# Splitting the last 2048 columns of one weight load into rows of 96, 20 and 12 partitions, and issuing four small loads ahead of the opening barrier

## Chip, cores, metric

One core of a Trainium2 chip. The metric is the device time of one execution in microseconds (us). Intervals are 95% intervals.

## The reference, cut

One decode step of a gated mix: attention of 32 query heads over 4 key/value heads with 65,536 cached positions, and a small gMLP mixer.

```python
q = (x @ wq)...; scores = einsum(q, k) * Dh ** (-0.5); p = softmax(scores)
a = einsum(p, v) @ wo                      # k_cache, v_cache: 4 x 65536 x 128 bf16 each
z = gelu(x @ w_in); z1, z2 = z[:Fh], layernorm(z[Fh:])
b = (z1 * (w_sp @ z2 + b_sp)) @ w_out      # w_out: 1792 x 1024
out = g * a + (1 - g) * b                  # g = sigmoid((x * gate_w).sum())
```

Some 162 MB have to be read for a result of 1,024 numbers.

Of the kernel before, what the change touches and what calls it, by code (L numbers as in the profile page):

```python
# [18 lines left out]
def handle_set(handle):  # L19
    return OrderedEngineSet([handle.engine])  # L20


class Recorder:
# [4 lines left out]
    def __init__(self):  # L28
        self.ops = []
        self.writer = {}  # L30
        self.readers = {}
        self.dma_count = {}
        self.ahead = 0
        self.at = None

    def op(self, eng, fn, r=(), w=(), dma=None, chan=None, take=()):
        o = Op()
        o.eng, o.fn, o.inc, o.count = eng, fn, False, 0
        o.dma, o.chan, o.take = None, chan, take
        o.at = self.at if eng == "PE" else None  # L40
        deps = {}
        for k in r:
            if k in self.writer:
                deps[id(self.writer[k])] = (self.writer[k], True)
        for k in w:
            if k in self.writer:
                deps.setdefault(id(self.writer[k]), (self.writer[k], False))
            for x in self.readers.get(k, ()):
                deps.setdefault(id(x), (x, False))
        o.deps = list(deps.values())  # L50
        for k in r:
            self.readers.setdefault(k, []).append(o)
        for k in w:
            self.writer[k] = o
            self.readers[k] = []
        if dma is not None:
            self.dma_count[dma] = self.dma_count.get(dma, 0) + 16
            o.dma = (dma, self.dma_count[dma])
        o.idx = len(self.ops)
        self.ops.append(o)  # L60
        return o
# [56 lines left out]
    def emit(self, nc):  # L118
        waits = self.plan()
        sems = {e: nc.alloc_semaphore("eng_" + e) for e in self.ENGINES}  # L120
        dsem = {k: nc.alloc_semaphore("dma_%s" % k) for k in self.dma_count}
        final = {k: v for k, v in self.dma_count.items()}

        csem = {c: nc.alloc_semaphore("chan_" + c) for c in {o.chan for o in self.ops if o.chan and o.dma is None}}
        csem.update({o.chan: dsem[o.dma[0]] for o in self.ops if o.chan and o.dma})
        step = {o.chan: 16 if o.dma else 1 for o in self.ops if o.chan}

        def one(o, ws, handle):
            for d in ws:
                if d.dma:  # L130
                    handle.wait_ge(dsem[d.dma[0]], d.dma[1])
                else:
                    handle.wait_ge(sems[d.eng], d.count)  # L133
            for c in o.take:
                handle.wait_ge(csem[c], step[c]).then_inc(csem[c], -step[c])  # L135
            last = o.fn(handle)
            if o.dma:
                last.then_inc(dsem[o.dma[0]], 16)
            elif o.chan:
                last.then_inc(csem[o.chan], 1)  # L140
            elif o.inc:
                last.then_inc(sems[o.eng], 1)

        def run(eng, handle):
            todo = [(o, ws) for o, ws in zip(self.ops, waits) if o.eng == eng]
            looped = [x for x in todo if x[0].at]
            n0 = todo.index(looped[0]) if looped else len(todo)
            assert all(x[0].at for x in todo[n0:n0 + len(looped)])
            for x in todo[:n0]:
                one(*x, handle)  # L150
            if looped:
                parts = {}
                for x in looped:
                    parts.setdefault(x[0].at, []).append(x)
                outer = 1 + max(k[0] for k in parts)
                inner = 1 + max(k[1] for k in parts if k[1] != "end")
                for o in range(outer):
                    for i in [-1] + list(range(inner)) + ["end"]:
                        p, q = parts[(o, i)], parts[(0, min(i, 0) if i != "end" else i)]
                        assert [x[0].take for x in p] == [x[0].take for x in q]  # L160
                with handle.bass.Fori(0, outer, engines=handle_set(handle), head_slot={handle.engine: 0}):
                    for x in parts[(0, -1)]:
                        one(*x, handle)
                    with handle.Fori(0, inner):
                        for x in parts[(0, 0)]:
                            one(*x, handle)
                    for x in parts[(0, "end")]:
                        one(*x, handle)
            for x in todo[n0 + len(looped):]:
                one(*x, handle)  # L170

        body = nc.cur_bb.bb
        gate = next(i for i, x in enumerate(body.instructions)
                    if isinstance(x, mybir.InstDrain) and x.engine == mybir.EngineType.SP)
        first = len(body.instructions)
        run("SP", nc.sync)
        nc.sync.wait_ge(dsem["out"], final["out"])
        made = list(body.instructions)
        moved = made[first:first + self.ahead]
        assert all(isinstance(x, mybir.InstDMACopy) for x in moved)  # L180
        body.instructions = made[:gate] + moved + made[gate:first] + made[first + self.ahead:]
        run("POOL", nc.gpsimd)
        run("ACT", nc.scalar)
        run("DVE", nc.vector)
        run("PE", nc.tensor)


def bass_gated_mix__gqa_block_cached__mixer_gmlp__decode_kernel(
# [45 lines left out]
    OFF = {}  # L234
# [16 lines left out]
    arena = nc.alloc_sbuf_tensor("arena", [128, NA], BF16)  # L251
# [51 lines left out]
    R = Recorder()  # L303
    P = R.op
# [48 lines left out]
    stream = []  # L353
# [1 line left out]

    GRAN = 1024

    def load(keys, src, off, chan=None):

        n = len(stream)  # L360
        w = src.shape[1]
        for i, key in enumerate(keys):
            place[key] = (n, off + i * (w // len(keys)), w // len(keys))
        stream.append((keys, off, src, chan))

    def rows(w, i, c):

        return w[128 * c * i:128 * c * (i + 1), :].rearrange("(p c) n -> p (c n)", c=c)
# [10 lines left out]
    VB = KR * SUB  # L379

    def load_k(n, slot):
        load([("k", n)], kv(A_k_cache, n), slot * SUB)

    def load_k2(n, slot):
        load([("k", n), ("k", n + 1)], kv(A_k_cache, n, True), slot * SUB)

    def load_v2(n, off, chan=None):
        load([("v", n), ("v", n + 1)], kv(A_v_cache, n, True), off, chan)
# [3 lines left out]
    load([("win", 0)], rows(B_w_in, 0, 8), VB)  # L392
    load_k(2, 2)
    load_k(3, 0)
    load([("wout", 0)], rows(B_w_out, 0, 14), VB)
    for i in range(6):
        a = 2 * i + 4
        if i % 3 == 2:
# [17 lines left out]
    def store():  # L416
        P("SP", lambda e: e.dma_start(out[0, 0].rearrange("(q n) -> q n", n=QW), osrc), r=["orow"],
          w=["out"], dma="out")
# [5 lines left out]
    def grains(off, w):  # L424
        return list(range(off // GRAN, (off + w + GRAN - 1) // GRAN))

    def issue():

        while issued[0] < len(stream):
            n = issued[0]  # L430
            keys, off, src, chan = stream[n]
            w = src.shape[1]
            gr = grains(off, w)
            if any(k not in used for x in gr if x in owner for k in owner[x]):
                return
            for j, x in enumerate(gr):
                owner[x] = (keys[j * len(keys) // len(gr)],)
            if n == len(stream) - 1:
                store()
            P("SP", lambda e, o=OFF["RING"] + off, w=w, src=src: e.dma_start(arena[:, o:o + w], src),  # L440
              w=[("slot", x) for x in gr], dma=chan or "s%d" % gr[0], chan=chan)
            issued[0] += 1

    def use(key):
        n, off, w = place[key]
        assert n < issued[0], key
        return arena[:, OFF["RING"] + off:OFF["RING"] + off + w], [("slot", x) for x in grains(off, w)]

    def done(key):
        used.add(key)  # L450
        issue()

    issue()


# [8 lines left out]
      r=["m32"], w=["sel"])  # L464
    P("DVE", lambda e: e.tensor_reduce(mq, vw(idf, 0, [[1, 16], [16, 8]]), AXX, ALU.add), r=["idf"], w=["mq"])
    P("DVE", lambda e: e.tensor_reduce(mhalf, vw(idf, 0, [[32, 2], [64, 2], [1, 32]]), mybir.AxisListType.XY, ALU.add),
      r=["idf"], w=["mhalf"])
# [4 lines left out]
    for fe in range(4):  # L472
        P("POOL", lambda e, fe=fe: e.tensor_copy(vw(sele, 128 * fe, [[32, 4], [1, 32]]),
                                                vw(idb, 64 * (fe // 2) + fe % 2, [[0, 4], [2, 32]])),
          r=["idb"], w=[KSE])
# [5 lines left out]
    def f(e):  # L481
# [7 lines left out]
      r=["oneb", "wsp", "bsp"], w=["mb"])  # L489
# [6 lines left out]
      r=["ones", "gs"], w=[KTB])  # L496
# [4 lines left out]
      r=["g"], w=["omg"])  # L501
# [3 lines left out]
    wqs, keys = use(("wq", 0))  # L505
# [354 lines left out]
    store()  # L860

    R.ahead = 2
    R.emit(nc)


# [26 lines left out]
```

## The kernel before, where the change touches it

All big loads stand in one list, `stream`. SP issues them in that order, each as one copy to all 128 partitions, as soon as the buffer is free. Each instruction is recorded with what it reads and writes; waits follow from that.

```python
def load(keys, src, off, chan=None):
    n = len(stream)
    w = src.shape[1]
    for i, key in enumerate(keys):
        place[key] = (n, off + i * (w // len(keys)), w // len(keys))
    stream.append((keys, off, src, chan))

def rows(w, i, c):                 # c rows of the weight side by side in a partition
    return w[128 * c * i:128 * c * (i + 1), :].rearrange("(p c) n -> p (c n)", c=c)
# ... cut ...
load([("wout", 0)], rows(B_w_out, 0, 14), VB)          # 128 rows of 28,672 bytes
# ... cut ...
P("SP", lambda e, o=OFF["RING"] + off, w=w, src=src: e.dma_start(arena[:, o:o + w], src),
  w=[("slot", x) for x in gr], dma=chan or "s%d" % gr[0], chan=chan)
```

SP's first two loads are moved ahead of the opening barrier already (`R.ahead = 2`). ACT issues four small loads (two of 8 rows of 256 bytes, two scalars of 2 bytes) after it.

## Time and profile before

| | before |
|---|---|
| median of the first 3 runs | 381.98 us (381.87 to 382.19) |
| span of the profiled run | 380.3 us |
| bytes read | 162.01 MB |
| DMA share, 96 to 375 us | 1.00 |
| first part of the last output-weight block lands | 376.48 us |

The profile page has one row per engine in 40 slices, then the DMA queues with packets, megabytes and their share of 16 engines' time. The chain of waits goes back from the last instruction. A table of time windows (the prediction calls them stretches) gives busy times of each engine, then granted clock, DMA share and GB/s. It counts a packet where it starts, so short windows can show a share over 1. Engines go by short names: SP (SyncE, which issues the big loads), ACT (ScalarE), PE (TensorE), DVE (VectorE), POOL (GpSimd).

Where this text speaks of packet records, they are the trace's list of DMA packets: start, duration, size. I speak of the *stretch* of a run: the sum, over the big loads' packets that start between 84 and 90 us, of duration minus the usual duration of that size (2,420 ns for 65,536 bytes, 1,062 for 28,672, 912 for 24,576, 159 for 4,096, 84 for 2,048, 9 for a completion packet of 4). It sums over the sixteen engines, so 16 engine-microseconds are 1 us for each. The kernel before has 0.7 engine-microseconds of it. The records don't name the engine of a packet; where a packet is put down to an engine, it was found by following ends to starts.

### The profile page before, as it was taken

The page shows a single profiled execution, that of the slowest core. Times are in us where ns is not written, and L with a number is a line of the kernel's source. Part 1 is how long each engine was busy: PE and PEld are TensorE (multiplying, and loading weights), DVE is VectorE, ACT ScalarE, POOL GpSimd, SP SyncE. Part 2 cuts the span into 40 slices and gives each one's busy share as a digit, 9 for nine tenths or more (in the row PEclk, how much of TensorE's full clock was granted, in tenths as well). Part 3 has the DMA queues.
Part 4 walks back from the last instruction along what each step waited for, and adds up shares of the span by engine and source line. Part 5 has one row for each costly group of instructions (what it writes and reads, how often), then busy time and mean ns, then how long its engine had stood idle before and what let it go on. Part 6 is the DMA issues. An engine that isn't in the chain of part 4 may idle for free. (4 is left out here: it accounts for less than half of the span.)

```text
span 380.3 us, 2726 instructions
## 1 busy us (share of the span) xinstructions
PE 236.0 (62%) x1477; PEld 60.7 (16%) x861; DVE 205.7 (54%) x166; ACT 23.2 (6%) x24; POOL 8.5 (2%) x39
## 2 busy tenths in 40 slices
PE   0050488466648934895787238953995784649386
PEld 0010011011201210121112001111111111212024
DVE  3111597778379625965892248745874882312020
ACT  1000000010400020002001100020002000220010
POOL 5000000000000000000000000000000000000000
PEclk9997599798959995999699758985899898959789
DMA  9998999999999999999999999999999999999995
GB/s 441 441 420 379 469 388 438 441 490 411 402 415 441 441 441 434 441 396 427 479 441 441 441 414 414 414 441 441 441 424 420 458 441 434 441 400 433 400 433 242
DMA packets 4251, 162.11 MB, mean 426 GB/s; under 512 B 533, under 2 KB 533, under 8 KB 789
## 3 DMA queue, kind: packets, MB, share of 16 engines
q1 hardware_dynamic: 4208, 162.01, 98.9%
q8 instruction: 5, 0.08, 0.1%
q10 hardware_dynamic: 36, 0.00, 0.0%
q14 instruction: 2, 0.01, 0.0%
HBM read 162.01 MB, written 0.00 MB: 426 GB/s over the span
## 5 line engine op out<-in xcount | busy, mean ns | idle before, releaser
L552 DVE STREAM_TRANSPOSE arena<-arena 128x2048 f32<-128x2048 f32 x64 | 143.1, 2285 | 43.9 <-DMA arena<-in_A_k_cache_dram 29.1
L309 PE MATMUL scp<-arena 128*128 128x512 bf16 (+1 forms) x275 | 111.2, 421 | 81.9 <-PEq L135 55.1
L311 PE MATMUL scp<-arena 128*128 128x512 bf16 (+1 forms) x279 | 111.1, 417 | 0.0
L309 PE MATMUL obt<-arena 128*64 128x512 bf16 (+3 forms) x337 | 64.2, 412 | 18.4 <-DMA arena<-in_A_v_cache_dram 11.2
L311 PE MATMUL obt<-arena 128*64 128x512 bf16 (+3 forms) x337 | 63.7, 409 | 0.0
L309 PEld LDWEIGHTS scp<-arena 128*128 128x128 bf16 (+1 forms) x275 | 27.5, 103 | 194.1 <-issue 170.5
L604 DVE STREAM_TRANSPOSE arena<-arena 128x2048 bf16<-128x2048 bf16 x7 | 16.2, 2311 | 30.7 <-PE obt L311 28.6
L309 PEld LDWEIGHTS obt<-arena 128*64 128x64 bf16 (+2 forms) x337 | 19.0, 111 | 69.2 <-issue 62.5
L599 ACT ACTIVATE arena<-arena 128x2048 bf16<-128x2048 f32 x8 | 16.0, 2002 | 218.5 <-DVE arena L596 112.8
L575 DVE TENSOR_SCALAR_CACHE_REDUCE arena<-scp 128x2048 f32<-128x2048 f32 x8 | 18.3, 2292 | 16.5 <-PE scp L311 16.5
L657 PE MATMUL mbt<-arena 128*128 128x128 bf16 x16 | 1.9, 260 | 14.5 <-PEq L135 13.4
L638 DVE RECIPROCAL arena<-mbt 128x1 f32<-128x1 f32 x4 | 0.6, 139 | 15.8 <-PE mbt L645 15.8
L607 DVE STREAM_TRANSPOSE arena<-arena 128x1024 bf16<-128x1024 bf16 x2 | 2.5, 1246 | 12.0 <-PE obt L311 12.0
L596 DVE TENSOR_REDUCE arena<-mbt 128x1 f32<-128x32 f32 x4 | 0.8, 192 | 14.4 <-PE mbt L591 14.4
L541 POOL COPY arena<-arena 32x32 bf16<-32x32 bf16 x16 | 3.2, 203 | 235.9 <-PE scp L311 210.8
L483 PE MATMUL scp<-arena 8*128 8x1 bf16 x8 | 0.6, 197 | 10.9 <-DVE arena L478 10.9
L488 PE MATMUL mbt<-arena 1*128 1x2 bf16 x1 | 0.2, 158 | 10.6 <-DMA arena<-in_B_b_sp_dram 10.6
L490 DVE COPY arena<-mbt 128x2 f32<-128x2 f32 x1 | 0.2, 160 | 10.5 <-PE mbt L488 10.5
L859 DVE CAST arena<-fbt 36x128 bf16<-36x128 f32 x1 | 0.3, 282 | 10.1 <-PE fbt L789 10.1
L789 PE MATMUL fbt<-arena 128*32 128x128 bf16 x128 | 4.0, 219 | 1.6 <-DMA arena<-in_A_wo_dram 1.6
L789 PEld LDWEIGHTS fbt<-arena 128*32 128x32 bf16 x128 | 3.6, 97 | 3.1 <-DMA arena<-in_A_wo_dram 1.6
L591 PE MATMUL mbt<-arena 128*128 128x1 f32 x28 | 4.1, 250 | 0.0
(95 smaller groups left out, 58.8 us busy)
## 6 DMA issues: line engine op xcount, KB each, us to landing
arena<-in_A_k_cache_dram SPq DMA_DIRECT2D x6, 4096.0 KB, 32.2
arena<-in_A_v_cache_dram SPq DMA_DIRECT2D x2, 4096.0 KB, 26.3
arena<-in_B_w_in_dram SPq DMA_DIRECT2D x1, 7168.0 KB, 30.8
arena<-in_A_wo_dram SPq DMA_DIRECT2D x3, 2048.0 KB, 33.5
arena<-in_B_w_out_dram SPq DMA_DIRECT2D x1, 3584.0 KB, 21.7
arena<-in_A_wo_dram SPq DMA_DIRECT2D x1, 1280.0 KB, 31.2
arena<-in_A_wo_dram SPq DMA_DIRECT2D x1, 512.0 KB, 31.8
arena<-in_A_wo_dram SPq DMA_DIRECT2D x1, 256.0 KB, 31.5
```

The lines of the kernel that those rows point to most:

```text
L309: return e.matmul(*a, **kw)
L311: one = e.matmul(*a, **kw).ins
L541: P("POOL", lambda e, pb=pb: e.tensor_copy(vw(qpad, 24 + 32 * pb, [[QP, 4], [1, 8]], 32 * pb, 32), vw(qall, 8 * g, [[32, 4], [1, 8]], 32 * ...
L552: P("DVE", lambda e: e.transpose(ktb(i).bitcast(F32), sl[:, 4096 * p:4096 * (p + 1)].bitcast(F32)), r=keys[4 * p:4 * p + 4], w=[("kt", i % ...
L575: P("DVE", lambda e: e.tensor_scalar(scs(j), scp[:, :], 0.0, None, op0=ALU.add, op1=ALU.max, accum_out=maxc[:, j:j + 1]), w=[("sc", j % 2) ...
L591: ins = e.matmul(mb[:, 32:33], bm, lp[:, h:h + 1], start=False, stop=(h == 1), skip_group_check=True)
L596: P("DVE", lambda e: e.tensor_reduce(gcol(g, K_NB), mb[:, 0:32], AXX, ALU.min), w=[("nb", g), "mb"])
L599: P("ACT", lambda e: e.activation(psb2, scs(j), ACTF.Exp, bias=gcol(j // 2, K_NB), scale=SCALE, accum_out=lp[:, j % 2:j % 2 + 1]), r=[("sc ...
L604: P("DVE", lambda e: e.transpose(ptsb2, psb2), r=["psb"], w=[("ptsb", 0), ("ptsb", 1)])
L607: P("DVE", lambda e: e.transpose(ptsb(n), ab("PSB", 1024, 1024 * (n % 2))), r=["psb"], w=[("ptsb", n % 2)])
L657: ins = e.matmul(mb[:, 0:128], sel[:, 128 * c:128 * (c + 1)], osc[:, 128 * c:128 * (c + 1)], start=(c == 0), stop=(c == 3))
L789: ins = e.matmul(fb[32 * b:32 * (b + 1), 0:QW], ovz[:, z:z + 32], sl[:, o:o + QW], start=False, stop=(i == 3 and c == 7), tile_position=(0 ...
```

## The change

The intent is to level the sixteen DMA engines: the short rows should give five engines more bytes and the others fewer. (The prediction says "Despite its title": the diff touches neither the matmuls nor the loop.) Its core (the rest counts one completion per copy):

```diff
+        dst = arena[:, OFF["RING"] + off:OFF["RING"] + off + w]
+        parts = [(dst, src)]
+        if cut:
+            c, heights = cut
+            parts = [(dst[:, 0:w - c], src[:, 0:w - c])]
+            p = 0
+            for k, h in heights:
+                parts.append((dst[p:p + h, w - c:w], src[p:p + h, w - c:w].rearrange("(i j) n -> i j n", i=k)))
+                p += h
...
-    load([("wout", 0)], rows(B_w_out, 0, 14), VB)
+    load([("wout", 0)], rows(B_w_out, 0, 14), VB, cut=(2048, ((16, 96), (5, 20), (3, 12))))
...
+        gate = next(i for i, x in enumerate(made) if isinstance(x, mybir.InstDrain) and x.engine == mybir.EngineType.Activation)
+        moved = made[first:first + self.early]
+        body.instructions = made[:gate] + moved + made[gate:first] + made[first + self.early:]
...
     R.ahead = 2
+    R.early = 4
```

More of the change, by code (lines that the diff above doesn't have):

```diff
@@ L33, in __init__, with op @@
         self.ahead = 0
+        self.early = 0
         self.at = None
-    def op(self, eng, fn, r=(), w=(), dma=None, chan=None, take=()):
+    def op(self, eng, fn, r=(), w=(), dma=None, chan=None, take=(), parts=1):
         o = Op()
@@ L56, in op @@
         if dma is not None:
-            self.dma_count[dma] = self.dma_count.get(dma, 0) + 16
+            self.dma_count[dma] = self.dma_count.get(dma, 0) + 16 * parts
             o.dma = (dma, self.dma_count[dma])
@@ L137, in one @@
             if o.dma:
-                last.then_inc(dsem[o.dma[0]], 16)
+                for x in last if isinstance(last, list) else [last]:
+                    x.then_inc(dsem[o.dma[0]], 16)
             elif o.chan:
@@ L182, in emit @@
         run("POOL", nc.gpsimd)
+        first = len(body.instructions)
         run("ACT", nc.scalar)
+        made = list(body.instructions)
+        gate = next(i for i, x in enumerate(made) if isinstance(x, mybir.InstDrain) and x.engine == mybir.EngineType.Activation)
+        moved = made[first:first + self.early]
+        assert all(isinstance(x, mybir.InstDMACopy) for x in moved)
+        body.instructions = made[:gate] + moved + made[gate:first] + made[first + self.early:]
         run("DVE", nc.vector)
@@ L356, in bass_gated_mix__gqa_block_cached__mixer_gmlp__decode_kernel, with load @@
     GRAN = 1024
-    def load(keys, src, off, chan=None):
+    def load(keys, src, off, chan=None, cut=None):
         n = len(stream)
@@ L363, in load @@
             place[key] = (n, off + i * (w // len(keys)), w // len(keys))
-        stream.append((keys, off, src, chan))
+        dst = arena[:, OFF["RING"] + off:OFF["RING"] + off + w]
[7 more added lines that the diff above has]
+                p += h
+            assert p == 128
+        stream.append((keys, off, w, parts, chan))
     def rows(w, i, c):
@@ L430, in issue @@
             n = issued[0]
-            keys, off, src, chan = stream[n]
-            w = src.shape[1]
+            keys, off, w, todo, chan = stream[n]
             gr = grains(off, w)
@@ L439, in issue @@
                 store()
-            P("SP", lambda e, o=OFF["RING"] + off, w=w, src=src: e.dma_start(arena[:, o:o + w], src),
-              w=[("slot", x) for x in gr], dma=chan or "s%d" % gr[0], chan=chan)
+            P("SP", lambda e, todo=todo: [e.dma_start(dst, x) for dst, x in todo],
+              w=[("slot", x) for x in gr], dma=chan or "s%d" % gr[0], chan=chan, parts=len(todo))
             issued[0] += 1
```

## The prediction

> **What bounds the kernel now.** I read the page's slices first, then the queue lines, then the end of the chain of waits, and last the busy time by stretches, cut finely at the end.
>
> The page has one row that is full from the first slice to the last but one, and it is not an engine's:
>
> ```profile
> PE   0050488466648934895787238953995784649386
> ...
> DVE  3111597778379625965892248745874882312020
> ...
> DMA  9998999999999999999999999999999999999995
> ...
> q1 hardware_dynamic: 4208, 162.01, 98.9%
> q8 instruction: 5, 0.08, 0.1%
> q10 hardware_dynamic: 36, 0.00, 0.0%
> ```
>
> PE and DVE have slices at 2 to 5 tenths in the middle, and the DMA engines have none. Packets of the big loads (q1) alone fill 98.9% of sixteen engines' span. The stretches say it again, by stage:
>
> ```profile
> 96.00:375.00 279.00, 188.47 (x1135) 48.25 (x645) 154.07 (x106) 20.08 (x19) 2.44 (x12) 0.85 1.00 431
> ```
>
> From 96 to 375 us the DMA share is 1.00 at 431 GB/s. In the trace's packet records I counted how many packets were under way at each moment: from about 2 us to about 375 us it is never under 16. So no wait for a buffer starves the stream, and an instruction that starts earlier in that time buys nothing. The end is the start of the stream, plus what the slowest engine has in its ring, plus the tail, which the chain shows:
>
> ```profile
> 345.31 31.17 DMA arena<-in_A_wo_dram
> 376.48 0.14 issue
> 376.62 2.05 PE fbt L789 x64
> 378.66 0.03 issue
> 378.69 0.02 DVEq L133
> 378.71 0.04 issue
> 378.75 0.28 DVE arena L859
> ```
>
> The first part of the last block of output weights lands at 376.48 us; 64 matmuls, the copy and the store follow and cost 380.3 - 376.5 = 3.8 us. This landing needs all sixteen engines, so I asked how level they are at the end:
>
> ```profile
> 374.00:376.00 2.00, 1.87 (x43) 1.03 (x35) 0.00 (x0) 0.00 (x0) 0.00 (x0) 1.00 0.94 369
> 376.00:376.25 0.25, 0.00 (x0) 0.00 (x0) 0.00 (x0) 0.00 (x0) 0.00 (x0) 1.00 0.67 262
> 376.25:376.50 0.25, 0.00 (x0) 0.00 (x0) 0.00 (x0) 0.00 (x0) 0.00 (x0) 1.00 0.40 157
> 376.50:376.75 0.25, 0.13 (x6) 0.17 (x8) 0.00 (x0) 0.00 (x0) 0.00 (x0) 1.00 0.34 139
> 376.75:377.00 0.25, 0.25 (x14) 0.25 (x12) 0.00 (x0) 0.00 (x0) 0.00 (x0) 1.00 0.39 150
> 377.00:377.25 0.25, 0.25 (x17) 0.25 (x13) 0.00 (x0) 0.00 (x0) 0.00 (x0) 1.00 0.30 115
> 377.25:377.50 0.25, 0.25 (x16) 0.25 (x12) 0.00 (x0) 0.00 (x0) 0.00 (x0) 1.00 0.28 107
> 377.50:377.75 0.25, 0.25 (x18) 0.25 (x13) 0.00 (x0) 0.00 (x0) 0.00 (x0) 1.00 0.09 33
> ```
>
> The number before the last in a line is the DMA share. It falls to about 0.36 soon after 376.25, stays near 0.3 for a microsecond and is gone by 377.7: 0.36 x 16 = some 6 engines finish over a microsecond after the other 10. The shares after 376 sum to 0.25 x 2.47 = 0.62 us, so the mean engine finishes at 376.6 and the last near 377.7. Perfect levelling is thus worth about 1.1 us, 0.3% of the time. This is the ceiling of the main part of the change.
>
> The records of completions show how the six came about. The last transfer lands on 10 engines within 0.27 us and on the others 0.98, 1.38, 1.39, 1.41, 1.56 and 1.68 us after the first. At 21 us after the start all sixteen are within 0.42 us. One engine drops behind between 41 and 58 us, two more by 105 us, a fourth by 124 us, one near 345 us, one at 374 us. The instruction packets of 16,384 bytes start at 53.0, 99.6, 107.1, 342.9 and 374.3 us and took 0.92 to 1.08 us each, and one of 8,192 bytes comes at 87.7 us: each puts one engine behind for good.
>
> [...]
>
> **The change part by part.** Despite its title the diff leaves the matmuls and the loop as they are.
>
> Part A, the four small loads of ACT go ahead of the opening barrier. ACT reaches it at 0.13 us and issues its first load at 1.25 us, so they move up by about 1.1 us, and their packets by one or two rounds of 2.42 us. The last scalar's completion, at 21.35 us, holds PE's first matmul of the stage at 22.09 us, just after the query weights landed at 21.8 us; with it gone PE starts up to 1.7 us sooner. Then SP issues the next load at about 27 instead of 28.46 us. But the stream holds the key load until about 41 us and has no hole to fill: worth 0. The four issues (0.58 + 0.28 + 0.27 + 0.27 = 1.4 us) delay the barrier by some 0.6 us: 0 as well, for SP's first two loads are already ahead of it. If ACT's first issue disturbs SP's, the stream starts later by 0.1 to 0.3 us, and that would be paid in full.
>
> Part B, the 3,584 KB load is issued as four copies: 24,576 bytes of each of 128 rows, then the last 4,096 bytes of 96, 20 and 12 rows.[...] Median packets: 28,672 bytes 1,062 ns, 16,384 bytes 615 ns, 4,096 bytes 159 ns. Interpolated, 24,576 bytes take 615 + 447 x 8,192 / 12,288 = 913 ns. One engine had 8 x 1,062 = 8,496 ns. Now:
> engines 5 to 15: 8 x 913 + 6 x 159 = 8,258, so -0.24 us;
> engines 3 and 4: 8 x 913 + 10 x 159 = 8,894, so +0.40 us;
> engines 0 to 2: 8 x 913 + 14 x 159 = 9,530, so +1.03 us.
> A further completion is a packet of 9 ns: nothing. Three more issues at 0.33 us are SP's, which waits most of the time. If the late engines all lie in 5 to 15, the last ends at 1.68 - 0.24 = 1.44 us, and engines 0 to 2 at most at 0.27 + 1.03 = 1.30 us: the landing comes 0.24 us earlier. The end follows it, because the 64 matmuls run back to back from it. That the heights fit so well makes me think they were chosen so.
>
> Sum: A 0, B -0.24 us at best. I predict 381.9 us and not 381.7, for the rivals below are nearly all on the slow side.
>
> **The rivals.**
> (a) A late engine is among 0 to 2. It ends at 1.4 to 1.68 + 1.03 us, and the time grows by 0.7 to 1.0 us, to 382.7 to 383.0. Following packets from end to start, the engines of the first three instruction packets are among the eight that carry the 8-row loads, and not the one that carries the scalars[...]. That makes this possible; only the deliberate heights speak against it. I give it 0.25. On 3 or 4, the engine that is 0.98 late would end at 1.38 us, harmless; one that is 1.4 late at 1.8 us, +0.1 us.
> (b) The instruction packets move: SP has three more issues and ACT's come earlier[...]. One more packet costs one engine 1.06 us: nothing on an early engine, up to 1 us on a late one.
> (c) [...]If it halves both rates for 4 x 159 = 0.64 us at a time, engines 0 to 2 lose up to 1.27 us more, and the time grows by up to 0.9 us. No line speaks for it, and the 30 us of queue behind each load hides it unless it makes the last engine later.
> (d) The earlier start of PE removes a wait that matters. The full DMA row speaks against it: 0.
>
> **Range and chances.** The three runs before spread over 0.3 us. Best case -0.8 us (levelling plus a luckier fetch), bad case +1.0 us. That gives 381.2 to 382.9 us, eight times in ten. A change of 2% is 7.6 us, seven times what levelling could give or the worst rival take; only a stream that runs dry could do it, and nothing removes buffers or adds bytes. Faster 0.01, within 2% 0.98, slower 0.01.
>
> **What would show it.** Right: q1's bytes unchanged at 162.01 MB, 128 more packets of 4,096 bytes and 24 more completions in it; DMA row full; the landing in the chain near 376.3 us; after it fewer engines busy at 0.3 share for a shorter time. Part A: PE's first matmul before 22 us, and no change at the end. Wrong: a share under 1.00 between 10 and 370 us, a first data packet clearly after 1.0 us, the last engine later than 377.7 us (rival a or c), or a different number of instruction packets (b).

The sums stand on an estimate of mine. The program groups the 96, 20 and 12 rows by 16, 5 and 3; I took these for the numbers of engines, with the five among the sixteen and the three among the five. That gives 6 + 4 + 4 = 14 short rows for three engines ("0 to 2"), 6 + 4 = 10 for two ("3 and 4") and 6 for eleven ("5 to 15"), against 8 before. Engine numbers, here and in the expectations, are labels of such groups: no trace names an engine. With the packet times of the trace before (159 ns for a short row, 913 interpolated for 24,576 bytes; the trace after has 912), this came to +1.03, +0.40 and -0.24 us; the forecast's sum was A 0 and B -0.24 us at best. The 24 more completions are 16 + 5 + 3. What rival (c) means by "it" is a conjecture, not shown then, that the engines that write the 20 and 12 rows and other engines are in each other's way.

What the trace before does show of completions: 29 loads of 128 rows and two stores of 8 packets make q1's 4,208 packets, 29 x (128 + 16) + 2 x (8 + 8); ACT's two loads of 8 rows and two scalars make q10's 36, 2 x (8 + 8) + 2 x (1 + 1). So a load of 128 rows leaves 16 packets of 4 bytes, one of 8 rows 8, a scalar one. I read this as one completion packet for each engine that a copy ran on, and count engines so below.

## The result

| | before | after |
|---|---|---|
| median (lowest to highest, 6 runs) | 381.97 us (381.61 to 383.78) | 383.74 us (383.23 to 384.55) |
| ratio | | 1.0041, 1.0019 to 1.0062 |
| packets of the big loads | 4,208 | 4,374 |
| stretch, 84 to 90 us | 0.7 | 29.3 engine-us |
| first part of the last block lands (profiled runs) | 376.48 us | 379.25 us |

Ratios are the mean time of one kernel's runs over that of the other's runs of the same rounds, so not quite the ratio of the medians. The change is within 2%, but it is slower by 1.8 us by the medians, and outside the predicted range (381.2 to 382.9). The profiled run of after is the slowest of its six (384.55 us); it is 0.8 us longer than their median, while the mechanism below is in the trace of every run of the split (stretch 30.8, 25.8 and 33.7 engine-us in runs 2, 4 and 12).

The page after, the DMA rows:

```profile
DMA  9999999999999999999999999999999999999995
...
DMA packets 4416, 162.11 MB, mean 423 GB/s; under 512 B 570, under 2 KB 570, under 8 KB 954
...
q1 hardware_dynamic: 4374, 162.01, 98.7%
```

The same bytes, the row as full as before, and yet 423 in place of 426 GB/s: the engines are busy all the time and move less. Where? SP's own issues in order of time show it, before:

```profile
80.27 0.33 SPq L440 DMA_DIRECT2D arena<-in_A_k_cache_dram  x1
99.70 0.33 SPq L440 DMA_DIRECT2D arena<-in_A_v_cache_dram  x1
118.94 0.33 SPq L440 DMA_DIRECT2D arena<-in_A_k_cache_dram  x1
```

and after:

```profile
80.72 0.36 SPq L457 DMA_DIRECT2D arena<-in_A_k_cache_dram  x1
100.02 0.35 SPq L457 DMA_DIRECT2D arena<-in_A_v_cache_dram  x1
120.75 0.33 SPq L457 DMA_DIRECT2D arena<-in_A_k_cache_dram  x1
```

SP's issues wait mostly for PE's work on earlier data (before, 188.7 us in 11 waits and 109.8 us in 6). They are late by 0.45, 0.32, then 1.81 us. In between the split load has gone through the engines (it is issued at 65.7 us and its completions land from 86.1 to 90.6 us; before, from 85.6 to 87.2). The table of windows over that time, before and after (the last two numbers are DMA share and GB/s):

```profile
78.00:104.00 26.00, 17.23 (x104) 4.87 (x64) 17.37 (x27) 5.14 (x6) 0.81 (x4) 0.93 1.01 436
```

```profile
78.00:104.00 26.00, 17.09 (x104) 4.98 (x64) 17.44 (x27) 4.83 (x6) 0.81 (x4) 0.93 1.02 409
```

The share is full in both and the rate falls from 436 to 409 GB/s. 26 us x 27 GB/s = 0.7 MB, or 1.6 us at 436 GB/s. (Packets counted by their start make this rough.) In the packet records the 128 short packets have a median of 274 ns, not 159, and the 65,536-byte packets of the next load that start from 84.9 to 88.2 us take 3,055 to 3,705 ns, not 2,420. Before, of 31 such packets 30 take 2,418 to 2,426 ns, and one, beside an instruction packet, 3,080.

From there on the loss is carried to the end: in the landings of the last transfer the mean of the sixteen engines is 379.06 us in place of 377.10, 1.96 us later, and 29.3 / 16 is 1.83. The end of the chain after:

```profile
348.62 30.62 DMA arena<-in_A_wo_dram
379.25 0.14 issue
379.38 1.77 PE fbt L806 x56
381.15 0.03 issue
381.18 0.42 PE fbt L806 x8
```

and the windows at the end:

```profile
378.00:378.25 0.25, 0.25 (x8) 0.10 (x1) 0.00 (x0) 0.00 (x0) 0.00 (x0) 1.00 0.50 172
...
378.50:378.75 0.25, 0.25 (x2) 0.00 (x0) 0.00 (x0) 0.00 (x0) 0.00 (x0) 1.00 0.35 131
378.75:379.00 0.25, 0.17 (x1) 0.00 (x0) 0.00 (x0) 0.00 (x0) 0.00 (x0) 1.00 0.33 124
...
379.25:379.50 0.25, 0.12 (x5) 0.15 (x7) 0.00 (x0) 0.00 (x0) 0.00 (x0) 1.00 0.19 74
379.50:379.75 0.25, 0.25 (x14) 0.25 (x12) 0.00 (x0) 0.00 (x0) 0.00 (x0) 1.00 0.08 33
...
380.25:380.50 0.25, 0.25 (x16) 0.25 (x10) 0.00 (x0) 0.00 (x0) 0.00 (x0) 1.00 0.08 33
```

Before, all engines were done by 377.7 us. Now some 6 engines (0.35 x 16) run on at 378.5 us, and one alone (0.08 x 16 = 1.3) to past 380.25: the tail is longer, not level. In the completion records the last transfer spreads over 3.06 us, not 1.68. Half of the difference is not the split's: in the load before it (near 77 us) the completions spread over 2.2 us already, and over 1.5 in the kernel before.

### The profile page after: what moved, and what is told of

Its sections match the earlier page's. It is cut to its first block, busy times and chain, and to the rows that moved or that the text cites. A ratio compares the mean times of both kernels' runs of the same rounds, so it can differ in the third digit from the quotient of the medians.

```text
span 383.2 us, 2729 instructions
## 1 busy us (share of the span) xinstructions
PE 235.0 (61%) x1477; PEld 60.7 (16%) x861; DVE 205.7 (54%) x166; ACT 23.2 (6%) x24; POOL 8.5 (2%) x39
## 3 DMA queue, kind: packets, MB, share of 16 engines
q1 hardware_dynamic: 4374, 162.01, 98.7%
## 5 line engine op out<-in xcount | busy, mean ns | idle before, releaser
L317 PE MATMUL scp<-arena 128*128 128x512 bf16 (+1 forms) x275 | 109.6, 415 | 86.0 <-PEq L136 58.5
L319 PE MATMUL scp<-arena 128*128 128x512 bf16 (+1 forms) x279 | 109.8, 412 | 0.0
```

Of the source, the lines that this page charges most:

```text
L317: return e.matmul(*a, **kw)
L319: one = e.matmul(*a, **kw).ins
```

## The experiments

Three theories. **Partitions:** a copy of other than 128 rows sends engines to partitions that others are writing, and both slow down. This is a conjecture. The expectations call it the port theory; that is only a name, for no trace names a port, or which engine writes which partition (in run 8's, "the run" is run 7). **Levels:** the unequal shares themselves, 14, 10 and 6 rows, make a late engine later. **Short rows or early loads:** further copies, short rows, or ACT's early issues cost time in themselves. Every run had five rounds. The diffs are shortened to the lines that matter. All results were correct.

### 1. The early loads alone

```diff
-    load([("wout", 0)], rows(B_w_out, 0, 14), VB, cut=(2048, ((16, 96), (5, 20), (3, 12))))
+    load([("wout", 0)], rows(B_w_out, 0, 14), VB)
```

> Part A alone: the four small loads go ahead of the barrier, the output-weight load is one copy again. If part A costs nothing but the split does (main theory), the time is 381.7 to 382.3 us and the first 96 us show the same leaders as before. If the early loads are what made the last engine 0.7 us late at the first landing (rival), about half of the loss stays: 382.5 to 383 us.

Measured: 381.96 us against 381.84, ratio 1.001 (0.9997 to 1.0024); stretch 0.7. At most a quarter of a per cent; no loss is shown. The interval alone doesn't exclude the rival (half of the loss is a ratio of 1.002), but run 2 shows the whole loss without the early loads.

### 2. The split alone

```diff
-    R.early = 4
+    R.early = 0
```

> Part B alone: the split into 96, 20 and 12 rows, the small loads where they were. Main theory: the whole loss is here, 383.3 to 383.9 us, and packets that start between 84 and 90 us take some 30 engine-microseconds more than their usual length. Rival (part A carries the loss): 381.7 to 382.2 us.

Measured: 383.85 us, ratio 1.0051 (1.0037 to 1.0065); stretch 30.8; 4,374 packets. The loss is all here.

### 3. The same short rows as one copy of 128

```diff
-cut=(2048, ((16, 96), (5, 20), (3, 12)))    # and the source grouped
+cut=(2048, ((16, 128),))                    # source rows plain; early = 0
```

> The same last 4,096 bytes of each row as one copy of 128 rows on 16 engines[...]. Port theory[...]: no stretched packets, 382.0 to 382.3 us, +0.1 us for the short rows. Rival (short rows or a further copy are slow in themselves): stretched packets stay, 383 us or more.

Measured: 381.96 us, ratio 1.0002 (0.9988 to 1.0015); stretch 0.9; the short packets' median is 159 ns. Short rows and one further copy cost nothing that can be seen (the interval allows 0.6 us).

### 4. Short rows as 96 and 32, both on 16 engines

```diff
+cut=(2048, ((16, 96), (16, 32)))            # early = 0
```

> The short rows as 96 and 32 rows, both on 16 engines: 6 + 2 = 8 rows for each engine, so no engine has more bytes than before[...]. Port theory: stretched packets as in the change, at least 10 engine-microseconds, 382.7 to 383.7 us. Rival (the loss is the 14, 10 and 6 rows[...]): no stretched packets, 382.0 to 382.3 us.

Measured: 383.74 us, ratio 1.0043 (1.0029 to 1.0057); stretch 25.8; short packets 253 ns, the next big ones 2,952 to 3,531 ns. Its 4,368 packets are 4,208 + 128 + 32, and no copy in the trace before leaves more than 16 completions: so 16 for each short copy, both on 16 engines. This is the run that counts most: if the rows of a copy are shared evenly, every engine has the same bytes as before (6 + 2 = 8 short rows), nothing is unlevelled, and the loss is the change's. The levels theory can't explain it. (It has one short copy more than run 3; run 9 has as many, and its next big packets take at most 2,558 ns.) The window from 78 to 104 us in run 3 and in this one:

```profile
78.00:104.00 26.00, 18.10 (x102) 4.99 (x63) 17.07 (x27) 4.61 (x6) 0.82 (x4) 0.86 1.02 437
```

```profile
78.00:104.00 26.00, 18.19 (x102) 5.07 (x63) 17.54 (x27) 4.15 (x6) 0.82 (x4) 0.87 1.05 425
```

437 against 425 GB/s with the same work and a full share.

### 5 and 6. Useless rows to partitions 0 to 63, and to 64 to 127

The kernel before, plus two copies of 32 rows of 4,096 bytes from other weights into a free part of the same buffer, grouped in the program as 8 groups of 4.

```diff
+pieces = (8, 0, 32), (8, 32, 32)       # run 5: engines meant, first partition, rows
+pieces = (8, 64, 32), (8, 96, 32)      # run 6
+parts.append((arena[p:p + h, ...], extra[0:h, 0:c].rearrange("(i j) n -> i j n", i=k)))
```

> The kernel before, with two further copies behind the mixer's output weights: 32 rows of 4,096 bytes (of no use, into a free part of the same buffer) to partitions 0 to 31 and 32 more to partitions 32 to 63, each on engines 0 to 7. Port theory: [...]no packet is stretched (under 2 engine-microseconds of excess); engines 0 to 7 fall 8 x 0.159 = 1.27 us behind. As late engines are believed to be among them, the time grows by about 1.3 us, to 383.1. If all late engines are in 8 to 15: 381.8 to 382.

> The same two copies from the same source rows on the same engines, but to partitions 64 to 95 and 96 to 127[...]. Port theory: packets of both halves are stretched by some 20 engine-microseconds between 84 and 92 us, and the time grows by about 2.5 us, to 384.3[...]. Rival (the imbalance or the number of copies costs, not the partitions): as the run with partitions 0 to 63, within 0.3 us.

Measured: run 5 383.81 us, ratio 1.0049 (1.0032 to 1.0066), stretch 21.9; run 6 384.3 us, 1.0063 (1.0046 to 1.0081), stretch 21.0. I had expected no stretch in run 5: a miss. The reason is in the queue line of run 5:

```profile
q1 hardware_dynamic: 4304, 162.27, 98.8%
```

4,304 is 4,208 + 64 rows + 32 completions: by them the two copies ran on 16 engines each and not on 8. The grouping (8, 4) steps evenly through the source here; with gaps between the groups the completions are 16 (run 9). On sixteen engines both runs show the stretch (21.9 and 21.0), so the pair tells nothing apart. That run 6 came out at the expected 384.3 us is luck: the rows came on 16 engines and not on the eight meant.

The same count settles what the change itself did: 4,374 = 4,208 + 128 + 38, and 38 = 16 + 10 + 12. Meant were 16 + 5 + 3 = 24. The instructions in the program, built again, have plain lists of 96, 20 and 12 rows. The 96 rows left 16 (as in run 4), so 22 are left for the others; if the rows of a copy are shared evenly, only 10 and 12 make 22. By this estimate the 20 rows ran on 10 engines and the 12 on 12, and no engine had more than 6 + 2 + 1 = 9 short rows where 14 were meant: **the levelling that was meant never took place.**

### 7 and 8. The change's two unequal pieces as further copies

```diff
+pieces = (5, 0, 20), (3, 32, 12)       # run 7
+pieces = (5, 96, 20), (3, 116, 12)     # run 8
```

> The kernel before with the change's own two unequal pieces as further copies, 20 rows on 5 engines and 12 rows on 3, to partitions 0 to 19 and 32 to 43[...]. No stretched packets. Engines 0 to 2 fall 1.27 us behind, 3 and 4 fall 0.64 us behind. If the late engines are none of 0 to 4 (the guess that the heights were chosen so): within 0.2 us of before. If one of 0 to 2 is late (rival a of the prediction): plus 1.0 to 1.3 us; if one of 3 and 4: plus 0.5 to 0.7 us.

> The same two pieces to partitions 96 to 115 and 116 to 127, as in the change. Port theory: stretched packets, 6 to 14 engine-microseconds, and the time 0.4 us or more above the run[...]. Rival: as that run, within 0.2 us.

Measured: run 7 383.0 us, 1.0028 (1.001 to 1.0045), stretch 12.3; run 8 382.91 us, 1.0023 (1.0006 to 1.004), stretch 14.1. They agree, against my expectation, for the same reason: 4,262 packets are 4,208 + 32 + 22, so, by the same estimate, 10 and 12 engines each time. These four runs confirm only that such copies stretched the stream wherever they went (21.9, 21.0, 12.3 and 14.1 engine-us).

### 9 and 10. The same on eight engines, this time really

Source rows in groups of 4 out of each 8, so that the groups have gaps between them.

```diff
-extra[0:h, 0:c].rearrange("(i j) n -> i j n", i=k)
+extra[0:8 * k, 0:c].rearrange("(i j) n -> i j n", i=k)[:, 0:h // k, :]
+pieces = (8, 0, 32), (8, 32, 32)       # run 9
+pieces = (8, 64, 32), (8, 96, 32)      # run 10
```

> Again two further copies of 32 rows of 4,096 bytes to partitions 0 to 63, but from source rows in groups of 4 with gaps between, which can't be merged into one list of 32: so they should run on 8 engines and not on 16, as the packet count of the earlier runs says they did (128 + 16 completions fewer or more: q1 4,208 + 64 + 16 = 4,288 packets).[...] Port theory: no stretched packets (under 2 engine-microseconds from 84 to 92 us), engines 0 to 7 fall 1.27 us behind, time up by 0 to 1.3 us by where the late engines are. Rival (any copy of other than 128 rows stalls the stream): 10 or more engine-microseconds of stretch, and 383.5 us or more.

> The same source rows on the same 8 engines to partitions 64 to 127[...]. Port theory: stretch of some 20 engine-microseconds in both halves, and the time at least 0.6 us above the run with partitions 0 to 63, up to 1.3 us above. Rival: the two runs agree within 0.2 us.

The queue lines, run 9 and run 10:

```profile
q1 hardware_dynamic: 4288, 162.27, 98.6%
```

```profile
q1 hardware_dynamic: 4288, 162.27, 98.7%
```

4,288 = 4,208 + 64 + 16: 16 completions for two copies, so eight engines each. Same source, same number of engines, same bytes; only the partitions written differ.

| | run 9, partitions 0 to 63 | run 10, partitions 64 to 127 |
|---|---|---|
| time (ratio to before) | 383.11 us (1.0024, 1.0012 to 1.0036) | 385.16 us (1.0081, 1.0068 to 1.0094) |
| short packets, median | 164 ns | 314 ns |
| next 65,536-byte packet of the eight engines without short rows | 2,418 ns, all eight | 4,032 to 4,619 ns |
| stretch | 4.4 | 31.1 |

```profile
78.00:104.00 26.00, 17.75 (x102) 4.96 (x63) 17.09 (x27) 4.84 (x6) 0.81 (x4) 0.85 1.01 432
```

```profile
78.00:104.00 26.00, 18.34 (x102) 5.07 (x63) 17.02 (x27) 4.65 (x6) 0.82 (x4) 0.86 1.02 407
```

The first line is run 9's, the second run 10's. This is the partitions theory by itself. When the eight engines write the first 64 partitions, the other eight don't notice: their next big packet takes 2,418 ns. When they write the last 64, their short packets take twice as long (314 and not 164 ns) and the other eight lose 1.6 to 2.2 us each. (The last 64 aren't slow in themselves: in the kernel before, 30 of the 31 big packets that start from 84.9 to 88.2 us, on all engines, take 2,418 to 2,426 ns.) The times differ by 2.05 us, more than the 1.3 that I had expected at most. A reading that fits is that the other eight engines are writing the last 64 partitions at that time; the runs show that the two kinds of packets slow each other there, not which engine writes which partition, nor what they share.

Run 9 tells another thing: after the short rows 8 engines land within 0.46 us of each other, five from 1.35 to 1.79 us, and three at 2.48, 3.21 and 3.63 us. So the three engines that instruction packets had delayed by then are all among the eight that carried the short rows, in line with what the prediction's rival (a) had read from the packets. At 159 ns a row these eight would have got 8 x 0.159 = 1.27 us more, and the medians grew by 1.2 us; but in the traced run many of the later short packets took some 284 ns, and the 64 took 14.1 engine-us, 1.76 us for each of the eight (that run is 1.7 us over the median of before). These 4 engine-us, over the 2 that I had expected at most, I can't explain.

### 11. The same useless bytes as one copy of 128 rows

```diff
+pieces = ((16, 0, 128),)               # 1,024 columns; source rows plain
```

> The same number of useless bytes (262,144) as one further copy of all 128 rows, 2,048 bytes each, on 16 engines: [...]8 x 84 ns = 0.67 us more for each. Port theory: no stretch, time up by 0.6 to 0.8 us. Rival (bytes and short rows in themselves cost what the earlier runs with further copies showed): up by 2 us.

Measured: 383.48 us, ratio 1.0028 (1.0015 to 1.0041); stretch 9.3, most of it in the 2,048-byte packets themselves, which took about 143 ns on average and not 84. Half a miss: the big packets of the next load start at most 0.27 us slow (2,694 ns at most) where runs 5, 6 and 10 had over 1 us, but the time grew by 1.6 us by the medians, not 0.7. As run 3 had no such slow short packets with the mixer's own weights as source, the source of the useless rows may play a part; that stays open. It doesn't touch the pair 9 and 10, which share a source.

### 12. The split as it was meant

```diff
-cut=(2048, ((16, 96), (5, 20), (3, 12)))
+cut=(2048, ((16, 96),) + 4 * ((5, 5),) + 4 * ((3, 3),))     # early = 0
```

> The split as it was meant: 96 rows on 16 engines, then four copies of 5 rows and four of 3 rows, which can't run on more than 5 and 3 engines; early loads not moved. If the loss came only from the 20 and 12 rows having run on 10 and 12 engines (so that nothing was levelled), this brings the time back to 381.5 to 382 us. Port theory: the 96 rows[...] still stretch the stream: 383.5 us or more, and more than the split of the change, as engines 0 to 2 now get 14 rows.

Measured: 383.62 us, ratio 1.0041 (1.0028 to 1.0054); stretch 33.7; 4,384 packets = 4,208 + 128 + 16 + 20 + 12, so, by the completions, 5 and 3 engines now. The larger numbers of engines aren't what cost the time: on the meant ones it is lost as well. That it would be worse than the change was wrong in the time; no difference is shown.

| run | what | ratio to before | stretch, engine-us |
|---|---|---|---|
| 1 | early loads | 1.0010 | 0.7 |
| 3 | 128 short rows, 16 engines | 1.0002 | 0.9 |
| 4 | 96 + 32, level | 1.0043 | 25.8 |
| 2 | 96 + 20 + 12 as in the change | 1.0051 | 30.8 |
| 12 | 96 + 20 + 12, really on 5 and 3 | 1.0041 | 33.7 |
| 9 / 10 | 64 useless rows, to partitions 0 to 63 / 64 to 127 | 1.0024 / 1.0081 | 4.4 / 31.1 |

No version beat the kernel before. Whether any split by rows can help the late engines is not shown.

## Why the prediction was wrong, point by point

- **What bounds the kernel:** right. The stream is full throughout, and what is lost in it at 85 us is lost at the end (1.83 us for an engine on average there, 1.96 at the last landing).
- **Part A, 0:** right in the time (run 1), off in sizes. PE's first matmul of the stage came at 21.64 us, sooner by 0.45 us and not by up to 1.7, for the last scalar's completion moved only from 21.35 to 21.09 us; SP's next load came at 28.31 us, not at 27. The barrier was delayed by 0.9 us and not 0.6 (POOL's first clearing of the buffer at 2.16 in place of 1.25 us). The stream didn't start later: its first packet starts at 1.00 us, before at 1.01.
- **Part B, the shares 14, 10 and 6:** the first step that failed. I took the engine count from the program's grouping; by their completions the copies ran on 16, 10 and 12 engines (22 shared out as 10 and 12 by the estimate under runs 5 and 6). The forecast of 24 more completions was the test of it: 38 came.
- **Part B, -0.24 us:** the second and larger failure. I priced a row at the usual 159 ns whoever wrote it, and the next load at nothing. The short rows measured 274 ns, and the next big packet of 15 engines some 0.6 to 1.3 us more: 29.3 / 16 = 1.8 us for an engine on average, against a gain of 0.24. That is near the 1.8 us by which the medians differ; the traced run itself is 2.6 us over the median of before, as one engine ended 1.2 us after the next.
- **Rival (c), short rows in the way of others:** the conjecture was named and the size was not far off ("up to 0.9 us"), but I placed it in the 20 and 12 rows alone and wrote "no line speaks for it". Run 4 has no such two pieces, only 96 and 32 rows on 16 engines, and shows 25.8 engine-us where the change shows 29.3. That a queue of 30 us hides it was wrong: the stream is the bound here, and the 1.83 us were still there at the end.
- **Rival (a):** that late engines are among those that carry the further rows was possible (in run 9 the three late ones were among the eight with short rows), but with the shares that really ran it decided nothing.
- **Rival (b):** instruction packets of 16,384 bytes were five before and after, so their number is out; on which engines they fell is not on record.
- **Range:** its upper end, 382.9 us, was 0.8 us short. The chances (within 2%) held.

## What to carry to other kernels

The DMA stream was the bound here, and a copy to other than all 128 partitions wasn't a neutral way to shift bytes between engines: 96 + 32 rows cost 25.8 engine-us of stretch and a ratio of 1.0043 where 128 rows cost 0.9 and 1.0002 (runs 4 and 3), and what 64 further rows cost turned on the partitions they went to (run 10 against run 9: 31.1 against 4.4). Count completions (packets beyond the rows) to see on how many engines a copy really ran; the program's grouping doesn't tell it (two copies of 32 rows, grouped as 8 x 4: 32 completions in run 5, 16 with gaps in run 9). Before levelling engines by rows, run the level version of the split (here 96 + 32): it shows the price of the split without its purpose.
